# A retention layer and a two-layer network in one kernel: filler matmuls replaced by seven matmuls of the next product, twelve tiles made unit by unit, one scaling moved

## The chip, the cores and the metric

The kernel runs on one core of one Trainium2 chip. The time is device microseconds of one execution; what is compared is the median of several runs. Engines are named as the profile names them: PE (matrix engine; PEld its weight loads), DVE (vector), ACT (scalar), POOL (GpSimd) and SP, which here only issues DMAs.

## The reference

```python
# q, k, v: [4, 8, 768, 64] float32
gamma = 1.0 - 2.0 ** (-5.0 - np.arange(H))
for t in range(S):
    state = gamma * state + outer(k[:, :, t], v[:, :, t])      # per batch and head, 64 x 64
    y[:, :, t] = (1 / sqrt(D)) * (q[:, :, t] @ state)
x = y.transpose(0, 2, 1, 3).reshape(3072, 512)
h = x @ w_in                                                   # [3072, 2048]
g = maximum(h, 0) + alpha * minimum(h, 0)
out = g @ w_out                                                # [3072, 512] float32
```

## The kernel before

The 3072 tokens are cut into 12 *units* of 256 tokens (three to a batch entry, `u`), and two units make a *block* of 512 tokens (`n`, six of them). The recurrence over time is made chunkwise: a unit has two chunks (`c`) of 128 tokens, and all 8 heads are done as 4 pairs.

For a unit the steps are:

- `load` (L149 and L143, issued by SP): keys, queries and values from memory; `hold` makes the next load wait for a named earlier instruction (`held`).
- `rescale` (L169, on DVE or POOL): keys (t = 0) and queries (t = 1) times powers of gamma into the tile `kdq`; `cast_v` (L185): values into `vx`.
- `turn_pe` (L199 on PE, then an ACT copy L205), later `turn_dma`: transposes into `kq`.
- `score_mm` (L284): queries against keys in PSUM tiles `sca` and `scb`; `masks` (L301, later L297, on DVE): causal masking into `m`.
- `sum_mm` (L229): the sum over keys and values of each chunk, in PSUM tile `st`; `state` (DVE L251 or L254, POOL L255) adds it to the running state `tf`, and `state_copy` writes two half copies `tg`, on POOL (letter `g`, L270) or ACT (`a`, L268).
- `out_mm` (L319 with the state, L339 with the scores): the unit's output `y` in two PSUM banks; `take_y` (L357, ACT) evicts them into `xT`, the input of the network.

For a block the network's two products are:

- `ffn1` (L404): 16 tiles of 128 hidden columns; the four matmuls of a tile are 512 tokens wide ("wide"), or, for the first `apart` tiles, the tile is made separately for each unit of the block with 256 tokens ("narrow"), two tiles to a PSUM bank, all those of the first unit ahead of those of the second. ACT (L415, `hm`) and DVE (L417, `gt`) evict: the network's nonlinearity.
- `ffn2` (L442) for block 0: the 64 matmuls of the second product, in four groups of 16, each group reading one quarter of w_out. Later blocks use `ffn2_seven` (L490), a seven-product scheme on 2 x 2 parts with sums of weights (`w_sums`, L375, DVE) and of activations (`g_sums`, L388, DVE).

The order on each engine is the order in which the program is written; no scheduler moves anything. `ffn1` and `ffn2` are generators: `tick(gen, m)` issues the next m matmuls of one, so that matmuls of one stage are laid by hand between steps of another. `keep(m)` issues m matmuls on constants (`kps`, L96) whose result nobody reads. POOL also issues the loads of w_in (`get_wi`, four quarters, L576) and w_out (`get_wo`, four quarters, L580), at their place in its own order. `behind` makes one instruction wait for another.

The places that the change touches are the stretch from unit 1's scores to the start of block 0's first product, block 0's second product (`gen`) with block 1's first product (`half`) laid into it, and POOL's scaling of units 4 and 5.

Of the kernel before, what the change touches and what calls it, by code (L numbers as in the profile page):

```python
# [21 lines left out]
def kernel(  # L22
# [55 lines left out]
    mj = sbp.tile([128, 512], F16, tag="mj", name="mj")[:, 0:384]  # L78
# [14 lines left out]
    def keep(m, bank=7):  # L93
        pt = ps(bank, "kps")
        for i in range(m):
            nc.tensor.matmul(  # L96
                out=pt, lhsT=spin[:, 0:128], rhs=spin, start=True, stop=True
            )
# [92 lines left out]
    def turn_pe(u, hh, bank):  # L191

        kdq, kq, _ = unit(u)
        trb = ps(bank, "trb", F16, 1024)
        n = 0
        for t in range(2):
            for r in range(2):
                for p in (2 * hh, 2 * hh + 1):
                    nc.tensor.transpose(  # L199
                        out=trb[:, n : n + 128],  # L200
                        in_=kdq[:, t, r, 2 * p : 2 * p + 2, :].rearrange("p a d -> p (a d)"),
                        identity=ident,
                    )
                    n += 128
        nc.scalar.activation(  # L205
            out=kq.rearrange("p (x a) i -> p x a i", x=4)[:, :, 2 * hh : 2 * hh + 2, :],
            in_=trb.rearrange("p (x a i) -> p x a i", x=4, a=2),
            func=COPY,
            bias=0.0,
            scale=1.0,  # L210
        )
# [29 lines left out]
    def state(u, c, eng, copy="gg"):  # L241

        state_copy(state_sum(u, c, eng), copy)
# [15 lines left out]
    def state_copy(uct, copy="gg"):  # L259
        if uct is None:  # L260
            return
        u, c, t = uct
        tg = tgbuf[(2 * u + c) % len(tgbuf)]
        tgs[(u, 1) if c == 0 else (u + 1, 0)] = tg
        for a in range(2):
            o, i = tg[rows(a), :, rows(a)], t[rows(a)]
            if copy[a] == "a":
                nc.scalar.activation(out=o, in_=i, func=COPY, bias=0.0, scale=1.0)  # L268
            else:
                nc.gpsimd.tensor_copy(out=o, in_=i)  # L270
# [39 lines left out]
    def out_mm(u, banks, evict=True):  # L310
        _, kq, vx = prepped[u]
        ys = [ps(banks[0], "y0"), ps(banks[1], "y1")]
        inter = [(u, c) in tgs for c in range(2)]
        assert inter == [u % UPB > 0, True]

        for c in range(2):
            for p in range(NP):
                if inter[c]:
                    nc.tensor.matmul(  # L319
                        out=ys[c][:, 128 * p : 128 * p + 128],  # L320
                        lhsT=tgs[u, c][:, p, :],
                        rhs=kq.rearrange("p (t r a) i -> p t r a i", t=2, r=2)[
                            :, 1, :, p, rows(c)
                        ],
                        start=(p == 0),
                        stop=False,
                        skip_group_check=True,
                    )
        for p in range(NP):
            m2s = live[u, p // 2]  # L330
            for r in range(2):
                for c in range(2):
                    for a in range(2):
                        o = ys[c][rows(a), 128 * p : 128 * p + 128]
                        at, n = 256 * r + 128 * (p % 2), 128
                        if u >= SPLIT and r == 1:
                            at, n = 256 + 64 * (p % 2), 64
                            o = o.rearrange("p (r i) -> p r i", r=2)[:, :, 32:64]
                        nc.tensor.matmul(  # L339
                            out=o,  # L340
                            lhsT=vx[rows(c), 2 * p + a, r, :],
                            rhs=m2s[a][rows(c), at : at + n],
                            start=(r == 0 and p == 0 and not inter[c]),
                            stop=(r == 1),
                            skip_group_check=True,
                        )
        live[u] = ys
        if evict:
            take_y(u, (0, 1))

    def take_y(u, cs):
        n, ul = divmod(u, 2)
        if n not in xT:
            xT[n] = sbp.tile([128, 2, NP, U], F16, tag="xT", bufs=2, name=f"xT{n}")
        ys = live[u]
        for c in cs:
            nc.scalar.activation(  # L357
                out=xT[n][:, ul, :, 128 * c : 128 * c + 128].rearrange(
                    "k a (p r) -> k a r p", r=2
                ),  # L360
                in_=ys[c].rearrange("k (a r p) -> k a r p", r=2, p=64),
                func=COPY,
                bias=0.0,
                scale=1.0,
            )
# [24 lines left out]
    def ffn1(n, banks, apart=0):  # L390


        gt = sbp.tile([128, NFT, TB], F16, tag="gt", bufs=2, name=f"gt{n}")
        gts[n] = gt
        turns = [(f, 2, ul, ul + 1) for ul in range(2) for f in range(0, apart, 2)]
        rest = range(apart, NFT)
        if apart == 0:
            rest = [f + x for f in range(HF) for x in (0, HF)]
        turns += [(f, 1, 0, 2) for f in rest]
        for i, (f0, nf, lo, hi) in enumerate(turns):  # L400
            hps = ps(banks[i % len(banks)], "hps").rearrange("p (f t) -> p f t", f=nf)
            for f in range(nf):
                for hp in range(4):
                    nc.tensor.matmul(  # L404
                        out=hps[:, f, :].rearrange("p (u t) -> p u t", t=U),
                        lhsT=w_in_all[:, hp, 128 * (f0 + f) : 128 * (f0 + f) + 128],
                        rhs=xT[n][:, lo:hi, hp, :],
                        start=(hp == 0),
                        stop=(hp == 3),
                    )  # L410
                    if f < nf - 1 or hp < 3:
                        yield
            hm = sbp.tile([128, TB], FP, tag="hm", bufs=3, name="hm")
            hm = hm.rearrange("p (f t) -> p f t", f=nf)
            nc.scalar.activation(out=hm, in_=hps, func=RELU, bias=0.0, scale=-1.0)  # L415
            for f in range(nf):
                nc.vector.scalar_tensor_tensor(  # L417
                    out=gt[:, f0 + f, U * lo : U * hi],
                    in0=hm[:, f, :],
                    scalar=oma_sb[:, f0 + f : f0 + f + 1],  # L420
                    in1=hps[:, f, :],
                    op0=MULT,
                    op1=ADD,
                )
            if n > 0 and f0 in ((HF + 3, NFT - 1) if apart == 0 else (NFT - 1,)):

                lo = 0 if apart or f0 < NFT - 1 else 4
                hi = HF if f0 == NFT - 1 else 4
                g_sums(n, 0, lo, hi)
                g_sums(n, 1, lo, hi)  # L430
            yield
# [134 lines left out]
    def tick(gen, m=10**6):  # L566
        for _ in range(m):
            if next(gen, 1) == 1:
                return
# [4 lines left out]
    def get_wi(lo, hi):  # L574
        s = slice(128 * lo, 128 * hi)
        return nc.gpsimd.dma_start(out=w_in_all[:, :, s], in_=wi[:, :, s])  # L576
# [6 lines left out]
    V, G, A = nc.vector, nc.gpsimd, nc.scalar  # L583
# [3 lines left out]
    load(1, ("k0", "q0", "k1", "q1", "v0", "v1"))  # L587
    V.memset(spin, 1.0)  # L588
    V.memset(mi, 1.0)
    V.memset(mj, 1.0)  # L590
    V.memset(warm, 0.0)
    A.activation(out=warm, in_=warm, func=RELU, bias=0.0, scale=-1.0)

# [55 lines left out]
    take_y(0, (0,))  # L649
    cast_v(G, 1, 0, 4)  # L650
    cast_v(G, 1, 4, 8)
    state_copy(s01)
    score_mm(1, 0, (4, 5))
    masks(1, 0)
    turn_pe(1, 1, 1)
    take_y(0, (1,))
    keep(2, 0)
    sum_mm(1, (6, 7))
    state(1, 0, G, "ga")
    get_wi(8, 12)  # L660
    get_wi(12, 16)
    score_mm(1, 1, (0, 1))
    masks(1, 1)
    state(1, 1, G)
    keep(5, 6)
    get_wo(0)
    rescale(G, 2, 0, 0, 4)
    get_wo(1)
# [1 line left out]
    rescale(G, 2, 0, 4, 8)  # L670
    rescale(G, 2, 1, 4, 8)
    cast_v(G, 2)
    out_mm(1, (4, 5))
    gen = ffn1(0, (2, 3, 6, 7, 0, 1, 2, 3, 6, 7, 4, 5, 0, 1, 2, 3), apart=4)
    tick(gen)


    gen = ffn2(0, (0, 1, 2, 3), parts=4)
    half = ffn1(1, (6, 7, 4, 5, 4, 5, 0, 1, 2, 3, 0, 4, 5, 6, 7, 1), apart=8)
    turn_pe(2, 0, 5)  # L680
    tick(gen, 5)
    score_mm(2, 0, (6, 7))
# [1 line left out]
    load(3, ("k0", "q0", "k1", "q1", "v"))  # L684
    masks(2, 0, (1,))
    turn_pe(2, 1, 4)
    tick(gen, 8)
    score_mm(2, 1, (6, 7))
    sum_mm(2, (5, 4))
    state(2, 0, G, "ga")  # L690
# [10 lines left out]
    w_sums(0, 0, HF)  # L701
    tick(gen, 9)
    out_mm(2, (4, 5))
    tick(gen, 10)
    tick(half, 24)
    turn_pe(3, 0, 6)
    tick(half, 8)
    turn_pe(3, 1, 7)
    tick(gen, 9)
    score_mm(3, 0, (4, 5))  # L710
    masks(3, 0)
    sum_mm(3, (6, 7))
    state(3, 0, G, "ga")
    tick(gen, 8)
    score_mm(3, 1, (4, 5))
    masks(3, 1)
    state(3, 1, G)
    for f in (0, 4):
        for i in range(1, 4):
            gate = w_sums(i, f, f + 4)  # L720
    behind(rescale(G, 4, 0, 0, 8), gate)
    rescale(G, 4, 1, 0, 8)
    rescale(G, 5, 0, 0, 8)
    rescale(G, 5, 1, 0, 8)
    cast_v(G, 4)
# [92 lines left out]
```

## Time and profile before

| | |
|---|---|
| median of 3 runs | 204.94 us (203.43 to 205.25) |
| profiled execution | 203.86 us, span 202.2 us |
| PE busy | 194.0 us (96% of the span) |
| DVE busy | 154.5 us (76%) |
| ACT busy | 101.8 us (50%) |
| POOL busy | 85.2 us (42%) |
| `kps` matmuls (L96), 25 of them | 8.3 us |
| `hps` matmuls (L404), 432 of them | 84.3 us |

The span is the time from the first to the last instruction of the program in one profiled execution; the execution's own time is 1.7 us longer. Shares are of the span. The busy time of PE counts from the start of a matmul to its modelled end, and matmuls overlap, so the spacing of starts says more than the mean duration. In an answer on groups, a row gives line, engine, operation, tile written and tiles read, count, busy us and mean ns of one, and then the engine's idle time ahead of the group with what ended it. In a timeline a row gives the start, the length, and the count of like instructions in a row; square brackets hold the idle time before it and its releaser. In the chain a row gives start, length, and where that time went.

### The profile page before, as it was taken

The page shows a single profiled execution, that of the slowest core. Times are in us where ns is not written, and L with a number is a line of the kernel's source. Part 1 is how long each engine was busy: PE and PEld are TensorE (multiplying, and loading weights), DVE is VectorE, ACT ScalarE, POOL GpSimd, SP SyncE. Part 2 cuts the span into 40 slices and gives each one's busy share as a digit, 9 for nine tenths or more (in the row PEclk, how much of TensorE's full clock was granted, in tenths as well). Part 3 has the DMA queues.
Part 4 walks back from the last instruction along what each step waited for, and adds up shares of the span by engine and source line. Part 5 has one row for each costly group of instructions (what it writes and reads, how often), then busy time and mean ns, then how long its engine had stood idle before and what let it go on. Part 6 is the DMA issues. An engine that isn't in the chain of part 4 may idle for free.

```text
span 202.2 us, 5547 instructions
## 1 busy us (share of the span) xinstructions
PE 194.0 (96%) x2314; PEld 127.8 (63%) x2314; DVE 154.5 (76%) x247; ACT 101.8 (50%) x169; POOL 85.2 (42%) x100
## 2 busy tenths in 40 slices
PE   6688999999999999999999999999999999999993
PEld 2356645566474778744688644788544888544882
DVE  7695887645899999189998289995489984589851
ACT  2455776246387333466454466433466255466321
POOL 5189319390269553980066950076920260000000
PEclk9999999999999999999999999999999999999999
DMA  5999999699997698998995499990570011200014
GB/s 153 312 233 146 194 231 289 185 229 183 333 306 229 143 241 209 245 244 221 201 216 135 152 212 236 208 239 19 179 170 0 3 52 58 104 0 0 9 46 156
DMA packets 77560, 33.95 MB, mean 168 GB/s; under 512 B 43216, under 2 KB 77024, under 8 KB 77536
## 3 DMA queue, kind: packets, MB, share of 16 engines
q1 hardware_dynamic: 73136, 29.37, 54.8%
q0 software_dynamic: 4224, 4.19, 13.6%
q8 instruction: 18, 0.29, 0.6%
q10 hardware_dynamic: 176, 0.04, 0.2%
q14 instruction: 6, 0.05, 0.1%
HBM read 27.31 MB, written 6.29 MB: 166 GB/s over the span
## 4 chain that ended last, share of the span: by engine, by line
PE 81%; DMA 7%; DVE 3%; POOL 3%; issue 2%; SPq 2%; ACT 1%; DVEq 0%; POOLq 0%
PE hps L404 39%; PE ox L490 16%; PE oy L490 11%; PE ops L442 5%; DMA wout<-in_moe_w_out_dram 4%; DMA ks<-in_k_dram 3%; PE y L339 2%; PE y L319 2%; SPq L149 2%; PE sca L284 2%; POOL tf L255 1%; PE st L229 1%; PE oz L490 1%; DVE ss L254 1%; DVE m L301 1%
## 5 line engine op out<-in xcount | busy, mean ns | idle before, releaser
L404 PE MATMUL hps<-xT,win 128*128 128x512 f16 (+1 forms) x432 | 84.3, 355 | 0.0
L417 DVE SCALAR_TENSOR_TENSOR gt<-hm,oma,hps 128x512 f16<-128x512 f32 (+1 forms) x108 | 70.8, 685 | 13.4 <-ACT hm L415 7.7
L415 ACT ACTIVATE hm<-hps 128x512 f32<-128x512 f32 x96 | 57.3, 597 | 33.4 <-PE hps L404 31.2
L404 PEld LDWEIGHTS <-win 128*128 128x128 f16 x432 | 42.2, 98 | 39.9
L490 PEld LDWEIGHTS <-gs 128*128 128x128 f16 x320 | 31.0, 98 | 3.7
L255 POOL TENSOR_TENSOR tf<-ss,tab 128x256 f32<-128x256 f32 x16 | 12.2, 764 | 37.0 <-DVE ss L254 36.0
L490 PEld LDWEIGHTS <-gt 128*128 128x128 f16 x240 | 22.8, 98 | 4.6
L169 POOL TENSOR_TENSOR kdq<-ks,tab 128x1024 f16<-128x1024 f32 (+1 forms) x10 | 17.3, 1727 | 16.7 <-DMA ks<-in_k_dram 11.1
L506 ACT ACTIVATE cu<-ox 128x512 f32<-128x512 f32 (+1 forms) x18 | 9.5, 526 | 29.5 <-PE ox L490 29.4
L511 DVE TENSOR_TENSOR os<-oy,cu 128x512 f32<-128x512 f32 x14 | 9.6, 688 | 17.3 <-PE oy L490 10.2
L270 POOL CAST tg<-tf 64x256 f16<-64x256 f32 x29 | 14.0, 482 | 19.6 <-DVE tf L251 18.2
L169 POOL TENSOR_TENSOR kdq<-qs,tab 128x1024 f16<-128x1024 f32 (+1 forms) x13 | 21.1, 1623 | 0.6 <-DMA qs<-in_q_dram 0.4
L490 PE MATMUL ox<-wsum,gs 128*128 128x256 f16 x160 | 19.1, 273 | 0.0
L357 ACT ACTIVATE xT<-y 128x512 f16<-128x512 f32 x24 | 16.2, 741 | 5.0 <-PE y L339 4.8
L442 PE MATMUL ops<-wout,gt 128*128 128x512 f16 x64 | 15.2, 380 | 0.2 <-DMA wout<-in_moe_w_out_dram 0.2
L185 POOL CAST vx<-vs 128x1024 f16<-128x1024 f32 (+1 forms) x13 | 12.5, 971 | 4.6 <-DMA vs<-in_v_dram 4.6
L388 DVE TENSOR_TENSOR gs<-gt 128x1024 f16<-128x1024 f16 (+1 forms) x14 | 13.1, 934 | 0.3
L268 ACT ACTIVATE tg<-tf 64x256 f16<-64x256 f32 x11 | 4.6, 414 | 15.4 <-POOL tf L255 10.2
L205 ACT ACTIVATE kq<-trb 128x1024 f16<-128x1024 f16 x8 | 8.2, 1023 | 6.3 <-PE trb L199 6.2
L301 DVE TENSOR_TENSOR m<-sca,mi 128x512 f16<-128x512 f32 x12 | 8.2, 685 | 3.0 <-PE scb L284 3.0
L490 PE MATMUL ox<-wout,gt 128*128 128x256 f16 x80 | 10.4, 274 | 0.0
L96 PE MATMUL kps<-spin 128*128 128x512 f16 x25 | 8.3, 471 | 1.8 <-DVE spin L588 1.5
(54 smaller groups left out, 187.9 us busy)
## 6 DMA issues: line engine op xcount, KB each, us to landing
out_dram<-os SPq DMA_DIRECT2D x21, 256.0 KB, 2.8
qs<-in_q_dram SPq DMA_DIRECT2D x8, 512.0 KB, 5.6
ks<-in_k_dram SPq DMA_DIRECT2D x24, 128.0 KB, 3.3
vs<-in_v_dram SPq DMA_DIRECT2D x24, 128.0 KB, 4.9
ks<-in_k_dram SPq DMA_DIRECT2D x8, 256.0 KB, 5.2
qs<-in_q_dram SPq DMA_DIRECT2D x8, 256.0 KB, 5.2
win<-in_moe_w_in_dram POOLq DMA_DIRECT2D x4, 512.0 KB, 7.3
wout<-in_moe_w_out_dram POOLq DMA_DIRECT2D x4, 512.0 KB, 8.5
```

Of the source, the lines that this page charges most:

```text
L169: return eng.tensor_tensor(out=kdq[:, t, :, h0:h1, :].rearrange("p r h d -> p h r d"), in0=staged[u]["kq"[t]][:, h0:h1, :].rearrange("p h ...
L185: eng.tensor_copy(out=o, in_=i)
L255: eng.tensor_tensor(out=t, in0=ss, in1=dec, op=MULT)
L270: nc.gpsimd.tensor_copy(out=o, in_=i)
L301: i = nc.vector.tensor_tensor(out=m2.rearrange("p (r a i) -> p r a i", r=2, a=2), in0=live[u, hh][a].rearrange("p (r a i) -> p r a i", r=2 ...
L357: nc.scalar.activation(out=xT[n][:, ul, :, 128 * c : 128 * c + 128].rearrange("k a (p r) -> k a r p", r=2), in_=ys[c].rearrange("k (a r p) ...
L388: return nc.vector.tensor_tensor(out=o, in0=a, in1=b, op=op)
L404: nc.tensor.matmul(out=hps[:, f, :].rearrange("p (u t) -> p u t", t=U), lhsT=w_in_all[:, hp, 128 * (f0 + f) : 128 * (f0 + f) + 128], rhs=x ...
L415: nc.scalar.activation(out=hm, in_=hps, func=RELU, bias=0.0, scale=-1.0)
L417: nc.vector.scalar_tensor_tensor(out=gt[:, f0 + f, U * lo : U * hi], in0=hm[:, f, :], scalar=oma_sb[:, f0 + f : f0 + f + 1], in1=hps[:, f, :],
L442: nc.tensor.matmul(out=opss[tq], lhsT=gt[:, ft, 128 * tq : 128 * tq + 128], rhs=w_out_all[:, ft, :], start=(ft == 0), stop=(ft == NFT - 1),)
L490: nc.tensor.matmul(out=o[1][m], lhsT=lhs(f, m), rhs=rhs(f), start=(first and f == 0 and (m == 0 or o[0] is None)), stop=(f == HF - 1), ski ...
```

## The change

- Ahead of unit 1's product the five constant matmuls `keep(5, 6)` go. In their place stand the first seven matmuls of block 0's first product, all narrow and of unit 0.
- Of unit 1's output one half is evicted by DVE instead of ACT (`take_y` gets an engine).
- The two state copies of unit 0's second chunk are made by ACT instead of POOL, and later in the program; the third quarter of w_in is issued by POOL in their place, earlier than before. The memset of `mj` goes from DVE to POOL.
- Block 1's first product makes 12 tiles unit by unit instead of 8, with one bank of the list changed; 16 of its narrow matmuls are laid ahead of unit 3's scores.
- The matmuls of block 0's second product are laid out otherwise around unit 2: five ahead of its first transpose, six instead of eight after the second, seven instead of ten after its output.
- The scaling of unit 4's keys on POOL moves from behind the last of the `w_sums` to just after unit 3's first state; the scaling of unit 4's queries is now the one that waits for the `w_sums`.

```diff
-    def take_y(u, cs):
+    def take_y(u, cs, eng=None):
...
+            if eng is not None:
+                eng.tensor_copy(out=o, in_=i)
+                continue
...
-    V.memset(mj, 1.0)
+    G.memset(mj, 1.0)
...
     cast_v(G, 1, 4, 8)
-    state_copy(s01)
+    get_wi(8, 12)
     score_mm(1, 0, (4, 5))
     masks(1, 0)
     turn_pe(1, 1, 1)
     take_y(0, (1,))
+    state_copy(s01, "aa")
     keep(2, 0)
     sum_mm(1, (6, 7))
     state(1, 0, G, "ga")
-    get_wi(8, 12)
     get_wi(12, 16)
     score_mm(1, 1, (0, 1))
     masks(1, 1)
     state(1, 1, G)
-    keep(5, 6)
+    gen = ffn1(0, (2, 3, 6, 7, 0, 1, 2, 3, 6, 7, 4, 5, 0, 1, 2, 3), apart=4)
+    tick(gen, 7)
     get_wo(0)
...
-    out_mm(1, (4, 5))
-    gen = ffn1(0, (2, 3, 6, 7, 0, 1, 2, 3, 6, 7, 4, 5, 0, 1, 2, 3), apart=4)
+    out_mm(1, (4, 5), evict=False)
+    take_y(1, (0,))
+    take_y(1, (1,), V)
     tick(gen)
...
     gen = ffn2(0, (0, 1, 2, 3), parts=4)
-    half = ffn1(1, (6, 7, 4, 5, 4, 5, 0, 1, 2, 3, 0, 4, 5, 6, 7, 1), apart=8)
+    half = ffn1(1, (6, 7, 4, 5, 4, 6, 0, 1, 2, 3, 0, 4, 5, 6, 7, 1), apart=12)
+    tick(gen, 5)
     turn_pe(2, 0, 5)
     tick(gen, 5)
     score_mm(2, 0, (6, 7))
...
     turn_pe(2, 1, 4)
-    tick(gen, 8)
+    tick(gen, 6)
     score_mm(2, 1, (6, 7))
...
     out_mm(2, (4, 5))
-    tick(gen, 10)
+    tick(gen, 7)
     tick(half, 24)
     turn_pe(3, 0, 6)
     tick(half, 8)
     turn_pe(3, 1, 7)
+    tick(half, 16)
     tick(gen, 9)
     score_mm(3, 0, (4, 5))
     masks(3, 0)
     sum_mm(3, (6, 7))
     state(3, 0, G, "ga")
+    rescale(G, 4, 0, 0, 8)
     tick(gen, 8)
...
-    behind(rescale(G, 4, 0, 0, 8), gate)
-    rescale(G, 4, 1, 0, 8)
+    behind(rescale(G, 4, 1, 0, 8), gate)
     rescale(G, 5, 0, 0, 8)
```

More of the change, by code (lines that the diff above doesn't have):

```diff
@@ L356, in take_y @@
         for c in cs:
+            o = xT[n][:, ul, :, 128 * c : 128 * c + 128].rearrange("k a (p r) -> k a r p", r=2)
+            i = ys[c].rearrange("k (a r p) -> k a r p", r=2, p=64)
+            if eng is not None:
+                eng.tensor_copy(out=o, in_=i)
+                continue
             nc.scalar.activation(
[L358 to L361, printed above, removed]
+                out=o,
+                in_=i,
                 func=COPY,
```

## The prediction

> **What bounds the kernel now.** I read the page's spans, busy times and chain first, then the time between PE's instructions stretch by stretch, then the landings of the weights that the moved matmuls read.
>
> ```profile
> span 202.2 us, 5547 instructions
> PE 194.0 (96%) x2314; PEld 127.8 (63%) x2314; DVE 154.5 (76%) x247; ACT 101.8 (50%) x169; POOL 85.2 (42%) x100
> PE 81%; DMA 7%; DVE 3%; POOL 3%; issue 2%; SPq 2%; ACT 1%; DVEq 0%; POOLq 0%
> ...
> 33.17:47.94 14.77, 14.53 (x185) 9.39 (x182) 9.22 (x16) 7.40 (x12) 8.59 (x10) 1.00 0.99 202
> 67.63:84.40 16.77, 16.34 (x306) 14.17 (x304) 13.11 (x19) 6.50 (x11) 8.90 (x10) 1.00 0.94 228
> ```
>
> The first three lines are the page's span, PE's busy share and the chain that ended last; the other two are stretches of the busy times (start and end, length, then PE, PEld, DVE, ACT, POOL, the granted clock, the DMA share and GB/s). PE is the bound. Once it has work it hardly stops: it is idle 0.24 us of the 14.77 in which block 0's second product runs, and 0.43 of the 16.77 that follow block 1's first product. So a new order of the same matmuls can only win what PE idles, or what it spends on filler. The diff touches three places: the filler before unit 1's product, the second product of block 0, and the tail of block 1's first product.
>
> **Place 1, the filler before unit 1's product.** Timeline and chain around it, and the load of the first quarter of w_in (POOL's issue, then the time to its landing):
>
> ```profile
> 16.38 0.22 PE L284 MATMUL scb<-kq 64*64 64x128 f16 x1
> 17.02 0.61 POOL L255 TENSOR_TENSOR tf<-ss,tab 128x256 f32<-128x256 f32 x1 [0.25 <-DVE ss L254]
> 17.66 0.41 ACT L268 ACTIVATE tg<-tf 64x256 f16<-64x256 f32 x1 [0.89 <-POOL tf L255]
> 17.69 0.39 POOL L270 CAST tg<-tf 64x256 f16<-64x256 f32 x1
> 18.03 1.55 POOL L576 DMA_DIRECT2D win<-in_moe_w_in_dram  x2
> ...
> 16.92 1.24 PE kps L96 x5
> 18.16 0.45 PE y L319 x8
> 18.61 0.57 PE y L339 x32
> 19.18 13.97 PE hps L404 x80
> ...
> 10.52 0.94 POOL L576 DMA_DIRECT2D win<-in_moe_w_in_dram  x1
> DMA to landing us min/median/max: 7.6/7.6/7.6
> ```
>
> The scores of unit 1 end at 16.38 + 0.22 = 16.60. Unit 1's product (L319, L339) needs the state copies tg, the last of which ends at 17.69 + 0.39 = 18.08. Between them stand five matmuls on constants (kps), 1.24 us, until 18.16. The change takes these out and puts in the first seven matmuls of block 0's first product, half as wide. Their price, from other rows of the same shape:
>
> ```profile
> 43.20 2.78 PE L404 MATMUL hps<-xT,win 128*128 128x256 f16 x24
> 45.83 0.62 PE L199 MATMUL trb<-mi,kdq 128*128 128x128 f16 x8
> 47.16 0.61 PE L199 MATMUL trb<-mi,kdq 128*128 128x128 f16 x8
> 47.94 2.10 PE L442 MATMUL ops<-wout,gt 128*128 128x512 f16 x9 [0.17 <-DMA wout<-in_moe_w_out_dram]
> 84.40 13.81 PE hps L404 x64
> ```
>
> 24 narrow ones take 45.83 - 43.20 = 2.63 us, 0.110 each; a wide one takes 13.81 / 64 = 0.216. Seven are 0.77 us that need not run later, and if they fitted between 16.60 and 18.08 that would be the gain. But they read columns of w_in whose load is issued at 10.52 and lands 7.6 us later, at 18.1. Nothing in the diff stands ahead of that issue that could bring it forward: before it POOL only gains the memset of mj (below). So the new order is: wait from 16.60 to 18.12, seven matmuls to 18.89, the product 0.45 + 0.57 = 1.02 to 19.91, the other 73 matmuls 13.97 - 0.77 = 13.20 to 33.11. Before, they end at 19.18 + 13.97 = 33.15. **Gain: 0.04 us.** The wait for the weights takes the place of the filler; behind it on PE stands unit 1's product, and ACT and DVE wait for that to evict it. The bounds are 0 (each 0.1 us that the load lands later is paid in full) and 0.77 (it lands by 17.3). I take 0.04, from the row.
>
> Around it, at nothing while the cover holds. The state copies of unit 0 go from POOL to ACT, two of 0.41 us, into ACT's idle 0.89; without that hole, the copy at 17.66 and with it unit 1's product would be late by the overhang. In POOL's place the third w_in load is issued before the tf at 17.02 instead of at 18.03: it is 0.78 us (1.55 for two) and takes the place of two POOL copies of 0.39, so POOL reaches tf as before. One half of unit 1's eviction goes to DVE; the trace has no such copy there, the nearest rows are the two forms of the group below, 0.48 and 0.75 us. I take 0.75. Both halves are then done at 19.91 + 0.75 = 20.7, and the first matmul that reads them comes after nine more narrow ones, at 19.91 + 0.99 = 20.9. The memset of mj on POOL:
>
> ```profile
> 2.08 0.29 POOL L594 TENSOR_SCALAR_AFFINE_SELECT mi<-mi 128x128 f16<-128x128 f16 x1 [1.57 <-DVE mi L589]
> ```
>
> POOL sits idle 1.57 us ahead of this and waits for DVE's memset of mi, which stands ahead of the one that moves. The new one would have to exceed 1.57 us to cost; it sets 128x384 elements where the 128x128 select takes 0.29, so three times that, 0.87, is my estimate. DVE's next work needs landed keys, so what it saves is worth 0 to the path.
>
> **Place 2, the wait for w_out.** In the row of 47.94 PE waits 0.17 us for the third quarter of w_out. What issues it:
>
> ```profile
> 39.72 0.80 POOL L580 DMA_DIRECT2D wout<-in_moe_w_out_dram  x1
> DMA to landing us min/median/max: 8.2/8.2/8.2
> ```
>
> It lands at 47.9. Three matmuls of the second product now stand ahead of the sums of unit 2 that did not (5 + 5 + 6 against 5 + 8), and POOL issues this load after the state of unit 2. So the issue goes back 3 x 0.216 = 0.65 us, to 40.4, the landing to 48.55, and SP's loads of units 4 and 5, which are held behind it, go back too. Against that, 16 narrow matmuls (1.75 us) now stand after the transposes of 47.16 and ahead of the matmul that waits. It comes at 47.94 - 0.17 + 1.75 = 49.52, with 0.97 us to spare. **Gain: 0.17 us**, bounds 0 and 0.17 while the landing slips by less than 0.97 more. The keys of unit 3 are issued later as well (two groups of five matmuls now stand ahead of the first scores where one did), which is what could make it slip. Unit 2's eviction stays just covered:
>
> ```profile
> 40.46 0.64 PE L339 MATMUL y<-m,vx 64*64 64x128 f16 x32
> 41.13 1.34 ACT L357 ACTIVATE xT<-y 128x512 f16<-128x512 f32 x2 [1.37 <-PE y L339]
> ```
>
> It ends 41.13 + 1.34 - 41.10 = 1.37 us after the product; ten matmuls (2.16 us) covered it, now seven do (1.52).
>
> **Place 3, twelve tiles unit by unit.** Four more tiles are made in halves: 16 wide matmuls become 32 narrow ones, 16 x (2 x 0.110 - 0.216) = 0.06 us on PE. **Loss: 0.05.** For DVE:
>
> ```profile
> L417 DVE SCALAR_TENSOR_TENSOR gt<-hm,oma,hps 128x512 f16<-128x512 f32 x84 | 60.6, 745 | 8.8 <-ACT hm L415 3.2
> L417 DVE SCALAR_TENSOR_TENSOR gt<-hm,oma,hps 128x256 f16<-128x256 f32 x24 | 10.3, 476 | 4.6 <-ACT hm L415 4.5
> ```
>
> By these means four tiles cost 4 x (2 x 476 - 745) = 0.83 us more; 24 halves are busy only 10.3 us together, 0.43 each, so 0.46 is the lower end. A pair of half tiles is then 0.86 to 0.95 us of DVE against 8 x 0.110 = 0.88 on PE, so DVE about keeps pace, and the last four tiles (0.745 against 0.865) let it catch up before the end. I take 0.
>
> **Place 3, unit 4's keys.** The 16 narrow matmuls also push the masks of unit 3 and the w_sums back by 1.75 - 0.17 = 1.58 us, while what is left of block 1's product shrinks as much. POOL's scalings of units 4 and 5 hang on the last w_sums:
>
> ```profile
> 47.91 0.37 SPq L149 DMA_DIRECT2D ks<-in_k_dram  x1
> DMA to landing us min/median/max: 4.2/4.2/4.2
> ...
> 52.12 0.39 POOL L270 CAST tg<-tf 64x256 f16<-64x256 f32 x1 [6.69 <-DVE tf L251]
> 54.66 0.93 POOL L255 TENSOR_TENSOR tf<-ss,tab 128x256 f32<-128x256 f32 x1 [2.15 <-DVE ss L254]
> 59.08 1.90 POOL L169 TENSOR_TENSOR kdq<-ks,tab 128x1024 f16<-128x1024 f32 x1 [1.88 <-issue]
> 66.50 2.02 POOL L185 CAST vx<-vs 128x1024 f16<-128x1024 f32 x2
> ...
> 68.43 0.63 PE L229 MATMUL st<-vx,kdq 64*64 64x64 f16 x44
> ```
>
> POOL runs from 59.08 to 68.52, PE's sums of units 4 and 5 from 68.43. Left as it was, that row of work would start at 60.66 and end at 70.1, 1.5 us or more behind PE. The scaling of unit 4's keys, 1.90 us, now goes into POOL's idle 2.15: after the tg of 52.12 (now 53.7 to 54.1) and before the tf of 54.66 (now 56.24). It ends at 56.0, and its keys land at 47.91 + 4.2 + 0.65 = 52.8. So the rest ends at 70.1 - 1.86 (the starts in this row are 1.86 apart on average: (66.50 - 59.08) / 4) = 68.24 against a need of 68.3 for the first and 68.6 for the last sums. **Cost: 0**, bounds 0 and 0.3.
>
> One wait is left as it stands:
>
> ```profile
> 75.32 0.41 PE L339 MATMUL y<-m,vx 64*64 64x128 f16 x15 [0.43 <-DVE m L301]
> ```
>
> DVE gets there from the last evicted tile by the same instructions, so it moves with PE.
>
> **The sum**: 0.04 + 0.17 - 0.05 = 0.16 us less. The profiled execution took 203.86 us (span 202.2 and 1.7 around it), so 203.7. The median of the runs shown, 204.94, is 1.1 above it; off that, **204.8**.
>
> **The rivals.**
>
> *The weights are early after all.* If the load of w_in lands by 17.3, the whole 0.77 is won: 204.94 - 0.16 - 0.73 = 204.05. For it: one execution shows one landing, and the queue is shared with the loads of unit 1. Against: 0.8 us is a tenth of its whole flight. Chance 0.22.
>
> *The clock falls in the new hole (slower).* Without the filler PE stands still from 16.60 to 18.12.
>
> ```profile
> 1.52 4.24 PE L96 MATMUL kps<-spin 128*128 128x512 f16 x10 [1.52 <-DVE spin L588]
> 5.43:8.84 3.41, 2.28 (x36) 1.30 (x34) 1.75 (x4) 1.02 (x1) 0.00 (x0) 1.00 1.06 314
> 15.67:19.08 3.41, 2.86 (x92) 1.92 (x80) 2.13 (x5) 1.51 (x3) 3.03 (x7) 1.00 1.09 155
> ```
>
> Ten such matmuls at the start took 4.24 us, 0.42 each, and five at 16.92 took 1.24: PE starts at half rate. Back at half rate for as long as those ten, it would lose 4.24 - 10 x 0.216 = 2.1 us: 204.94 + 2.1 - 0.16 = 206.9. It decides as soon as the hole counts as rest. Against: PE was busy 2.28 of 3.41 us in the early stretch without falling; the hole, from 16.92 where the filler began, leaves 2.86 - 1.2 = 1.66 in its stretch, about half. Chance 0.1. The Trainium skill (TensorE: Matmul & The Clock Gate, Part 1: The HAM clock gate) says that the clock halves after an idle window of about 3.4 us, by which a hole of 1.5 would be harmless; its section on a second failure mode says that frequent short idles between groups make the clock swing, by which this rival holds. No run here shows which.
>
> *The late loads overtake the cover (slower by a little).* If w_out's third quarter slips 1 to 2 us more, or POOL's row ends late by its 0.3, PE waits 0.1 to 1.0: 204.9 to 205.8. For it: the issue goes back and meets later key loads. Against: 0.97 to spare. Chance 0.18.
>
> The forecast keeps 0.5.
>
> **How the numbers follow.** A measurement of this kernel can tell about 1% (2.05 us) from no change; the runs before spread over 1.8. No case for faster reaches 2.05, only a spread of runs on the early weights: 0.06. The clock case lies at the bound, so half of it and some of the late loads together: 0.1. Within 1%: 0.84. The range goes from the early weights less the spread of the runs below the median, 203.0, to the clock case, 206.9.
>
> **What would show it.** Right: no kps at 16.9, seven hps from 18.1 with an idle of about 1.5 us put down to win; the last matmul of block 0's first product at 33.1; no wait at the third w_out quarter, which lands near 48.6; a POOL scaling of ks between 54 and 56; the 0.43 us wait still there. Wrong: seven hps before 17.5 (early weights), hps 0.2 us apart after 18 (clock), a wait on wout at 49.5, or sums of unit 4 that wait for POOL.

## The result, and the profile after

| | before | changed |
|---|---|---|
| median (22 runs each) | 203.70 us (202.71 to 205.25) | 202.83 us (201.88 to 206.15) |
| ratio | | 0.9944, 95% interval 0.9921 to 0.9967 |
| profiled execution | 203.86 us, span 202.2 | 203.15 us, span 201.4 |

By the ratio the changed kernel is faster by 0.56%, 1.1 us; the forecast was 0.16 us, within what counts as no change here. The ratio leaves out three runs of the changed kernel in which PE's granted clock fell (0.989 to 0.992, 205.0 to 206.15 us); over all runs the medians lie 0.87 us apart. In a repeat of the changed kernel beside other kernels the ratio was 0.9936 (0.9897 to 0.9974).

The page of the changed kernel (span, busy times, chain that ended last):

```profile
span 201.4 us, 5574 instructions
PE 193.2 (96%) x2325; PEld 129.0 (64%) x2325; DVE 155.3 (77%) x251; ACT 102.0 (51%) x170; POOL 85.1 (42%) x99
PE 86%; DMA 6%; DVE 2%; POOL 2%; SPq 1%; issue 1%; ACT 0%; POOLq 0%
```

PE's busy time fell by 0.8 us although it issues eleven matmuls more on balance: five wide filler matmuls are gone. Place 1 in the timeline of PE (first two rows: the last of unit 1's scores, then the seven) and in the chain:

```profile
15.93 0.22 PE L284 MATMUL scb<-kq 64*64 64x128 f16 x1
17.72 0.94 PE L407 MATMUL hps<-xT,win 128*128 128x256 f16 x7 [1.57 <-DMA win<-in_moe_w_in_dram]
...
10.06 7.61 DMA win<-in_moe_w_in_dram
17.67 0.05 issue
17.72 0.94 PE hps L407 x7
18.66 0.45 PE y L319 x8
19.10 0.57 PE y L339 x32
19.67 13.20 PE hps L407 x73
```

This is the forecast's picture: the load is 7.61 us on its way, PE is idle 1.57 us for it, then come the seven, unit 1's product and 73 more in 13.20 us. Only the seven take 0.94 us in the chain where the forecast has 0.77. In this execution place 1 wins nothing. PE's timeline at place 2 and at its wait for a mask of DVE, then, for place 3, POOL's and the first sums of units 4 and 5:

```profile
46.85 0.61 PE L199 MATMUL trb<-mi,kdq 128*128 128x128 f16 x8
47.30 1.91 PE L407 MATMUL hps<-xT,win 128*128 128x256 f16 x16
49.04 2.11 PE L445 MATMUL ops<-wout,gt 128*128 128x512 f16 x9
74.72 0.41 PE L339 MATMUL y<-m,vx 64*64 64x128 f16 x15 [0.43 <-DVE m L301]
```

```profile
53.59 1.90 POOL L169 TENSOR_TENSOR kdq<-ks,tab 128x1024 f16<-128x1024 f32 x1
55.76 0.93 POOL L255 TENSOR_TENSOR tf<-ss,tab 128x256 f32<-128x256 f32 x1 [0.28 <-DVE ss L254]
60.19 1.90 POOL L169 TENSOR_TENSOR kdq<-qs,tab 128x1024 f16<-128x1024 f32 x1 [1.88 <-issue]
65.77 2.02 POOL L185 CAST vx<-vs 128x1024 f16<-128x1024 f32 x2
...
67.83 0.63 PE L229 MATMUL st<-vx,kdq 64*64 64x64 f16 x44
```

The group of 49.04 has no bracket: no wait for w_out is left here. Unit 4's keys are scaled in POOL's hole from 53.59, and POOL's row ends at 67.79, just ahead of PE's sums of units 4 and 5 from 67.83. PE's wait of 0.43 us for DVE stands as before. So each step can be seen, and yet the two traces explain only part of 1.1 us. Of the 0.71 us between the spans 0.45 lie ahead of every difference on the path: unit 1's scores end at 15.93 + 0.22 = 16.15 here and at 16.60 before. The experiments had to tell whether that, place 1 or place 2 made the median.

### The profile page after: what moved, and what is told of

Read it like the earlier page. It is cut to its first block, busy times and chain, and to the rows that moved or that the text cites. A ratio compares the mean times of both kernels' runs of the same rounds, so it can differ in the third digit from the quotient of the medians.

```text
span 201.4 us, 5574 instructions
## 1 busy us (share of the span) xinstructions
PE 193.2 (96%) x2325; PEld 129.0 (64%) x2325; DVE 155.3 (77%) x251; ACT 102.0 (51%) x170; POOL 85.1 (42%) x99
## 4 chain that ended last, share of the span: by engine, by line
PE 86%; DMA 6%; DVE 2%; POOL 2%; SPq 1%; issue 1%; ACT 0%; POOLq 0%
PE hps L407 41%; PE ox L493 16%; PE oy L493 11%; PE ops L445 7%; DMA win<-in_moe_w_in_dram 4%; PE y L339 3%; DMA vs<-in_v_dram 3%; PE y L319 2%; PE sca L284 2%; SPq L149 1%; PE st L229 1%; PE trb L199 1%; PE oz L493 1%; DVE gs L391 1%; POOL tf L255 1%
## 5 line engine op out<-in xcount | busy, mean ns | idle before, releaser
L407 PEld LDWEIGHTS <-win 128*128 128x128 f16 x448 | 43.5, 98 | 40.2 <-DMA win<-in_moe_w_in_dram 1.7
L493 PEld LDWEIGHTS <-gt 128*128 128x128 f16 x240 | 22.8, 98 | 4.6
L270 POOL CAST tg<-tf 64x256 f16<-64x256 f32 x27 | 13.2, 491 | 19.6 <-DVE tf L251 18.3
L362 ACT ACTIVATE xT<-y 128x512 f16<-128x512 f32 x23 | 15.7, 743 | 6.0 <-PE y L339 5.8
L268 ACT ACTIVATE tg<-tf 64x256 f16<-64x256 f32 x13 | 5.3, 414 | 14.0 <-POOL tf L255 9.0
L445 PEld LDWEIGHTS <-gt 128*128 128x128 f16 x64 | 5.8, 98 | 6.0
```

Source lines behind the costliest of these rows:

```text
L407: nc.tensor.matmul(out=hps[:, f, :].rearrange("p (u t) -> p u t", t=U), lhsT=w_in_all[:, hp, 128 * (f0 + f) : 128 * (f0 + f) + 128], rhs=x ...
L445: nc.tensor.matmul(out=opss[tq], lhsT=gt[:, ft, 128 * tq : 128 * tq + 128], rhs=w_out_all[:, ft, :], start=(ft == 0), stop=(ft == NFT - 1),)
L493: nc.tensor.matmul(out=o[1][m], lhsT=lhs(f, m), rhs=rhs(f), start=(first and f == 0 and (m == 0 or o[0] is None)), stop=(f == HF - 1), ski ...
```

## The experiments

Theory A: the gain lies at place 2, where a wait for w_out costs more than its idle time shows. Theory B, later sharpened to D: at place 1, in executions in which w_in lands earlier than in the two profiled ones. Theory C: in the start and the early loads. The traces also serve as a sample of when w_in lands.

**One place at a time.** `e1_seven` is the kernel before with place 1 alone:

```diff
-    state_copy(s01)
+    get_wi(8, 12)
...
+    state_copy(s01, "aa")
...
-    get_wi(8, 12)
...
-    keep(5, 6)
+    gen = ffn1(0, (2, 3, 6, 7, 0, 1, 2, 3, 6, 7, 4, 5, 0, 1, 2, 3), apart=4)
+    tick(gen, 7)
...
-    out_mm(1, (4, 5))
-    gen = ffn1(0, (2, 3, 6, 7, 0, 1, 2, 3, 6, 7, 4, 5, 0, 1, 2, 3), apart=4)
+    out_mm(1, (4, 5), evict=False)
+    take_y(1, (0,))
+    take_y(1, (1,), V)
```

> Kernel before with place 1 alone: the seven matmuls in the filler's stead, half of unit 1's eviction on DVE, the state copies on ACT and the third w_in load issued early; memset and second product as before. Theory A (the gain lies at place 2, where a wait for w_out costs more than its idle time shows): no gain here, 0.0 to 0.2 us slower, and in its trace the seven start within 0.1 us of the landing of w_in, some 1.5 us after the scores of unit 1. Theory B (the gain lies at place 1, in executions in which w_in lands early): 0.5 to 0.8 us faster, and the idle ahead of the seven under 1.0 us. Theory C (the gain lies in the early loads and the start): as much faster as the kernel with the early loads alone.

Measured: 0.9959 (0.9935 to 0.9982), 0.8 us faster. In its trace PE waits for the load only 0.57 us:

```profile
16.83 0.94 PE L407 MATMUL hps<-xT,win 128*128 128x256 f16 x7 [0.57 <-DMA win<-in_moe_w_in_dram]
17.61 0.61 PE L319 MATMUL y<-kq,tg 128*128 128x128 f16 x8
```

The gain and the idle are those of theory B; theory A's "no gain here" falls.

`e2_second` is the kernel before with everything from the start of `ffn2(0)` on as in the changed kernel (places 2 and 3; some of its lines):

```diff
-    half = ffn1(1, (6, 7, 4, 5, 4, 5, 0, 1, 2, 3, 0, 4, 5, 6, 7, 1), apart=8)
+    half = ffn1(1, (6, 7, 4, 5, 4, 6, 0, 1, 2, 3, 0, 4, 5, 6, 7, 1), apart=12)
...
+    tick(half, 16)
     tick(gen, 9)
...
+    rescale(G, 4, 0, 0, 8)
```

> Kernel before with places 2 and 3 alone: twelve tiles unit by unit, the second product laid out anew, unit 4's keys scaled early. Theory A: most of the measured gain, 0.3 to 1.1 us faster; no wait at the third w_out quarter in its trace. Theory B: 0.1 to 0.2 us faster at most. Theory C: the same.

Measured: 0.9972 (0.9948 to 0.9997), 0.57 us faster (0.06 to 1.1). Its trace shows no wait at the third w_out quarter. The prediction gives these places 0.17 - 0.05 = 0.12 us, which lies inside that interval; so A is not refuted for its part, and not shown by this time alone.

`e3_early` has only the moved loads, copies and memset:

```diff
-    V.memset(mj, 1.0)
+    G.memset(mj, 1.0)
...
-    state_copy(s01)
+    get_wi(8, 12)
...
+    state_copy(s01, "aa")
...
-    get_wi(8, 12)
```

> Kernel before with only the state copies on ACT, the third w_in load issued early and the memset of mj on POOL; filler and second product as before. Theory A and theory B: within 0.2 us of the kernel before. Theory C: 0.4 us or more faster, with the first transposes or the start of block 0's first product earlier by that in its trace.

Measured: 0.9987 (0.9963 to 1.0011), not told from nothing. Theory C has no support. But its trace shows no wait at the third w_out quarter either, nor does that of `e1_seven`, which moves the same loads and copies and keeps the old second product. So the moves, or chance in the landing, may share in what place 2 wins. The 0.8 of `e1_seven` contains them too, and the two parts together (0.41% and 0.28%) come to a little more than the whole.

**The kernels themselves again.** `e0_before` and `e10_before` are the kernel before, unchanged, and `e9_after` the changed kernel, unchanged, one profiled execution each; `e7_after` is the changed kernel once more, in 12 runs.

> The kernel before once more, for a second trace of it. If the 0.45 us by which the changed kernel's profiled execution was ahead at the scores of unit 1 are chance of the first loads, this trace lies anywhere between or beyond the two at that point, and its wait for the third w_out quarter differs from 0.17 us. If they belong to the change, this trace has the scores of unit 1 end near 16.6 us again.

> The kernel before for one more trace. Theory D: whenever w_in lands, block 0's first product ends 16.55 us after the scores of unit 1, since the filler and the state copies stand ahead of it; the PE work behind it takes 165.4 us plus the wait for the third w_out quarter, 0.2 to 0.45 us.

> The changed kernel for one more trace of the landing of w_in. Theory D: from the scores of unit 1 to the landing 0.3 to 0.6 us (two times in three) or 1.5 us, and the end of block 0's first product is 15.2 us plus that wait behind the scores, whichever it is.

> The changed kernel once more, beside the other three. Theory D: w_in lands within 0.7 us of the scores of unit 1 in its trace, the idle ahead of the seven is under 0.8 us instead of 1.57, and the median is 0.8 to 1.3 us below the kernel before. Theory A: the idle is near 1.5 us again and the gain is that of the second product alone, 0.3 to 0.6 us.

Measured: unit 1's scores end at 16.04 in `e0_before` and at 15.87 in `e10_before`, so the 0.45 us at the start is chance of the first loads and not the change. At the third w_out quarter the kernel before is not idle in `e0_before` and waits longest in `e10_before`:

```profile
46.52 0.61 PE L199 MATMUL trb<-mi,kdq 128*128 128x128 f16 x8
47.63 2.10 PE L442 MATMUL ops<-wout,gt 128*128 128x512 f16 x9 [0.49 <-DMA wout<-in_moe_w_out_dram]
```

The median of `e7_after` is 202.12 us, 1.45 under the kernel before beside it (1.3 by the ratio, 0.9936), and PE is idle 0.55 us ahead of the seven: theory D. The chain of `e7_after` beside that of the changed kernel's first trace above:

```profile
9.87 6.67 DMA win<-in_moe_w_in_dram
16.54 0.05 issue
16.59 0.94 PE hps L407 x7
17.52 0.46 PE y L319 x8
17.99 0.57 PE y L339 x32
18.56 13.20 PE hps L407 x73
```

The load takes 6.67 us instead of 7.61, unit 1's scores end 0.12 earlier, and block 0's first product ends at 31.75 instead of 32.87. From these traces, each read in the same way: S is the end of unit 1's scores, L the landing of the first quarter of w_in, F the end of block 0's first product, Z the end of PE's last matmul.

| kernel | L - S | F - S | Z - F |
|---|---|---|---|
| filler: first trace of before | 1.50 | 16.54 | 165.78 |
| filler: `e0_before` | 0.26 | 16.56 | 165.57 |
| filler: `e10_before` | 0.14 | 16.54 | 166.19 |
| filler: `e3_early` | 0.27 | 16.56 | 165.36 |
| filler: `e2_second` | 0.60 | 16.56 | 165.35 |
| seven: `e1_seven` | 0.53 | 15.72 | 165.36 |
| seven: first trace of changed | 1.52 | 16.72 | 165.35 |
| seven: `e7_after` | 0.51 | 15.72 | 165.36 |
| seven: `e9_after` | 0.80 | 15.99 | 165.39 |
| seven: `e8_two` (below) | 1.17 | 16.36 | 165.36 |

With the filler F - S is 16.55 whenever the weights land; with the seven it is 15.2 plus L - S, and 15.72 at best among these. `e9_after` was expected to keep to that sum, and does; its landing, 0.80, lies between the two values that were expected. The gain is 0.84 us at L - S = 0.5, nil at 1.35, and -0.17 at 1.5. Of the twelve traces in which the quarter is loaded whole (these ten, `e4_hole` with 1.56 and `e6_keys` with 0.51), eight have L - S at 0.8 or less: both traces that the comparison began with belong to the four others. What differs is the load itself: unit 1's scores end 6.1 to 6.4 us behind its issue in all twelve, while from issue to landing it takes 6.22 to 7.03 us in the eight and 7.25 to 7.64 in the four. Stretches of the changed kernel's first trace, then the same of `e7_after` (the last two columns are the DMA share and GB/s):

```profile
13.00:14.00 1.00, 0.84 (x49) 0.58 (x41) 1.00 (x2) 1.00 (x2) 1.00 (x2) 1.00 1.09 167
14.00:15.00 1.00, 1.00 (x17) 0.58 (x11) 1.00 (x3) 0.63 (x2) 1.00 (x3) 1.00 1.19 174
```

```profile
13.00:14.00 1.00, 0.92 (x51) 0.67 (x40) 1.00 (x3) 0.99 (x2) 1.00 (x2) 1.00 1.23 203
14.00:15.00 1.00, 1.00 (x19) 0.53 (x20) 1.00 (x3) 0.65 (x2) 1.00 (x3) 1.00 1.22 196
```

In the two stretches the core moves 167 and 174 GB/s instead of 203 and 196, at a DMA share of 1.09 and 1.19 against 1.23 and 1.22; why, the runs do not show. The last column of the table is place 2 but for 0.1 us or less: 0.2 to 0.8 us that all traces with its rearrangement or with the early loads lack. At the upper end, in `e10_before`, it is nearly twice the most that was expected of that trace.

**Nothing in the hole.** `e4_hole` is the changed kernel without the seven ahead:

```diff
     gen = ffn1(0, (2, 3, 6, 7, 0, 1, 2, 3, 6, 7, 4, 5, 0, 1, 2, 3), apart=4)
-    tick(gen, 7)
```

> The changed kernel with nothing in the filler's place: the five constant matmuls gone, the seven issued after unit 1's product with the rest. Theory D (in most executions w_in lands within 0.7 us of the scores of unit 1, so that the seven fill a wait of 1.4 us that unit 1's product has anyway): slower than the changed kernel by 0.5 to 0.8 us in the median. Theory A (place 1 is worth nothing, as in the profiled execution of the changed kernel): the same as the changed kernel within 0.2 us. The clock rival: with PE at rest for 1.4 us in every execution, some of them with a granted clock under 0.995 and 2 us longer; if the hole does not count as rest, no more of those than of the kernel before.

Measured: 202.86 us, ratio 0.9964 (0.9941 to 0.9986), against 202.12 and 0.9936 of the changed kernel beside it: 0.74 us in the median, theory D's figure, though the intervals of the two ratios overlap. The kernel with places 2 and 3 and the filler (`e2_second`) has 0.9972, so in the median the empty hole costs no more than the filler. But in the profiled execution the clock falls. Stretches before, during and after, the granted clock being the third figure from the end:

```profile
14.80:18.23 3.43, 2.05 (x81) 1.47 (x84) 2.43 (x5) 2.61 (x5) 3.04 (x7) 1.00 1.16 166
18.23:21.65 3.42, 3.42 (x39) 2.38 (x28) 1.20 (x3) 1.34 (x2) 2.15 (x4) 0.50 1.16 175
21.65:25.06 3.41, 3.41 (x26) 2.42 (x25) 2.73 (x8) 2.15 (x4) 0.00 (x0) 1.00 1.21 205
```

```profile
17.11 0.85 PE L319 MATMUL y<-kq,tg 128*128 128x128 f16 x8 [1.08 <-ACT tg L268]
...
17.58 0.38 PE y L319 x4
17.96 0.73 PE y L339 x32
18.69 15.42 PE hps L407 x80
```

Right behind the hole the granted clock is 0.50 for 3.4 us, and the 80 matmuls take 15.42 us instead of the 13.97 of before.

**The first load cut in two**, `e5_split`:

```diff
-    get_wi(0, 4)
+    get_wi(0, 2)
     rescale(G, 1, 1, 0, 4)
+    get_wi(2, 4)
...
-    held.append(get_wi(4, 8))
-    load(2, ("k0", "q0", "k1", "q1", "v"))
...
     cast_v(G, 1, 4, 8)
-    get_wi(8, 12)
+    held.append(get_wi(4, 8))
+    load(2, ("k0", "q0", "k1", "q1", "v"))
...
+    get_wi(8, 12)
     get_wi(12, 16)
```

The second quarter, unit 2's loads and the third quarter move back with it.

> The changed kernel with the first w_in load cut in two: the two tiles that the seven read come alone, the other two after the first scaling of unit 1's queries, the second quarter after unit 1's values are cast. Theory D: the seven wait for no load in any trace; the median 0.1 to 0.4 us lower than the changed kernel's, and the spread of its runs smaller at the top. Theory A: no difference. Against both: POOL is 0.8 us longer before unit 1's state, and if that is on the path, 0.3 to 0.8 us slower.

Measured: 202.36 us, 0.9927 (0.9898 to 0.9955). The median is 0.24 above that of the changed kernel beside it, where 0.1 to 0.4 below was expected, and the ratio is a little under its 0.9936: the two are not told apart. Its highest run is 203.02 against 204.58. The seven wait for no load, but PE does, twice, further on:

```profile
16.33 0.92 PE L407 MATMUL hps<-xT,win 128*128 128x256 f16 x7 [0.21 <-ACT xT L362]
21.61 0.60 PE L407 MATMUL hps<-xT,win 128*128 128x512 f16 x2 [0.23 <-DMA win<-in_moe_w_in_dram]
38.08 1.24 PE L445 MATMUL ops<-wout,gt 128*128 128x512 f16 x5 [0.44 <-DMA wout<-in_moe_w_out_dram]
```

The wait is moved, not removed: w_in's second quarter and w_out's second quarter come later.

**Unit 4's keys back behind the w_sums**, `e6_keys`:

```diff
-    rescale(G, 4, 0, 0, 8)
     tick(gen, 8)
...
-    behind(rescale(G, 4, 1, 0, 8), gate)
+    behind(rescale(G, 4, 0, 0, 8), gate)
+    rescale(G, 4, 1, 0, 8)
```

> The changed kernel with the scaling of unit 4's keys behind the last of the w_sums again, ahead of unit 4's queries. By the prediction's own step POOL's row of work ends about 1.9 us later, at 69.6 on the changed kernel's trace, and PE waits 1.2 to 1.6 us for it at the sums of units 4 and 5: 1.2 to 1.6 us slower than the changed kernel. If DVE's work after block 1's first product hides part of it (PE waits there 0.43 us anyway), 0.5 to 1.1 us slower.

Measured: 205.53 us, 1.0081 (1.0046 to 1.0116), 3.4 us above the changed kernel beside it, twice the larger expectation, with a granted clock of 0.989 to 0.992 in all five runs.

```profile
67.48 0.45 PE L229 MATMUL st<-vx,kdq 64*64 64x64 f16 x32 [0.80 <-POOL vx L185]
69.46 0.37 PE L229 MATMUL st<-vx,kdq 64*64 64x64 f16 x11 [1.53 <-POOL vx L185]
```

```profile
66.25:69.66 3.41, 1.08 (x51) 0.78 (x51) 3.27 (x4) 0.19 (x1) 3.15 (x3) 1.00 0.68 154
69.66:73.07 3.41, 3.41 (x58) 2.58 (x51) 3.28 (x6) 0.38 (x1) 1.96 (x4) 0.50 0.77 176
```

PE waits 0.80 and 1.53 us for POOL's two casts, and then the clock is at half for 3.41 us, which costs half of that, 1.7; the later wait of 0.43 us for DVE is gone. So the cover was needed: without it places 2 and 3 together lose.

**Two filler matmuls ahead of the seven**, `e8_two`, meant to shorten the hole:

```diff
+    keep(2, 2)
     gen = ffn1(0, (2, 3, 6, 7, 0, 1, 2, 3, 6, 7, 4, 5, 0, 1, 2, 3), apart=4)
     tick(gen, 7)
```

> The changed kernel with two of the constant matmuls back, ahead of the seven. Theory D: they take 0.43 us of a wait that is at least 0.5 us long, so the median stays within 0.15 us of the changed kernel's (0.5 to 0.7 % under the kernel before). Clock rival: if it is the hole that makes the clock fall in some executions of the changed kernel (and of the one with nothing in the filler's place), the shorter hole shows fewer runs with a granted clock under 0.995, none of some twelve. If the filler delays the seven, 0.2 to 0.4 us slower.

Measured: 202.31 us, 0.9955 (0.9928 to 0.9981), 0.45% under the kernel before where 0.5 to 0.7 was expected: not told from the changed kernel. None of its 12 runs has a granted clock under 0.995. Of the 34 timed runs of the changed kernel four have, of 12 of `e4_hole` one, of 12 of `e1_seven`, which has the same hole, none; of the 73 runs of the kernel before that were timed beside the experiments one has, of the 24 of `e2_second` and `e3_early`, both with the filler, none. That points to the hole, but the numbers are small. No version tried is shown to beat the changed kernel.

## Why the prediction was wrong, step by step

- **Place 1, "I take 0.04, from the row": the step that failed.** The mechanism was right, the wait for the weights does take the filler's place. But one execution's landing, 18.1, was taken for the kernel's, and it was a late one: 1.50 us behind the scores, where eight of twelve traces have 0.8 or less. In the traces of kernels with the seven that land so, the term is 0.56 to 0.84 instead of 0.04; place 1 alone, with the moved loads, gave 0.8 us (`e1_seven`, 0.4 to 1.3), and the seven against an empty hole 0.74 with overlapping intervals (`e4_hole`). The rival "the weights are early after all" had it, with a chance of 0.22 where about two in three was due. Its objection, that 0.8 us is a tenth of the flight, was no argument: flights of 6.67 and 7.61 us both occur. Nor is a shared queue the reason: on the page the loads of w_in stand under POOL's queue and those of the units under SP's.
- **The sum at place 1 was off even for a landing at 18.1.** It starts unit 1's product at 18.16, the modelled end of the filler, but prices the seven by the spacing of starts, 0.77. From start to modelled end they take 0.94; counted alike, that landing costs 0.13 instead of winning 0.04. The first trace of the changed kernel, landing 1.52 us behind the scores, shows a loss of 0.17.
- **Place 2, 0.17: too small.** The gap in the row runs from the modelled end of the last transpose. By starts it is more: the transposes of 47.16 are followed after 0.78 us by the waiting matmul, those of 46.85 after 0.45 by the next, so 0.33 was lost. And it varies with the landing of w_out: in `e10_before` the idle is 0.49 us. From the table the whole stretch behind F is 0.2 to 0.8 us shorter; how much of that the rearrangement won and how much the early loads, the runs do not tell apart. The predicted slip of the issue to 40.4 is 39.95 with the 0.45 by which this execution is ahead; the trace has 40.06, and no wait took its place.
- **Place 3, narrow matmuls and DVE**: right. Block 1's remaining product runs from 58.17 to 66.87, 8.70 us; 48 narrow and 16 wide at the prediction's prices are 8.7. PE's wait of 0.43 us for DVE stayed.
- **POOL's cover**: right that it is needed; "1.5 us or more behind PE" was short of the 3.4 us that its loss costs, since the clock falls on top.
- **The clock rival**: its mechanism exists, read in two traces, and three of the 22 runs of the changed kernel have a mean granted clock of 0.989 to 0.992 like those two; it did not set the median. By the Trainium skill's rule (TensorE: Matmul & The Clock Gate, Part 1: The HAM clock gate) it takes an idle window of about 3.4 us. The length agrees with the 3.41 and 3.42 us at half clock here, but the condition does not: PE was busy for 2.05 of 3.43 us in `e4_hole` before the clock fell.
- **The range and the signs.** 202.83 lies below 203.0, the low end. The median of before over more runs is 203.70 instead of the 204.94 on which the range stood, so 1.2 of the 2.0 us between 204.8 and 202.83 are the base and 0.7 the two terms. The low end does not follow from its own words either: the early weights, 204.05, less the spread of the runs below the median, 204.94 - 203.43 = 1.51, is 202.5.

## What to carry to other kernels

A landing read from one trace is one draw. Where a step is worth its full price or nothing by a microsecond of a transfer, take more than one trace of the landing, or give the two outcomes their own chances, before one row sets the sum. Filler ahead of a wait is the first place to put real work, as long as that work's own inputs are there; and a wait's price is read from start to start, not from the idle time alone.

## What the runs showed of the hardware

The clock can fall without a stretch of full rest. Stretches of 3.41 us, in step with the clock's own changes in each trace: it fell after PE had been busy for 1.08 us (`e6_keys`) and 2.05 us (`e4_hole`, whose row above is 3.43 long), then ran at 0.50 for one such stretch and came back. But it held after 1.90 us in the changed kernel's first trace, in the stretch that has most of its hole of 1.57 us, and after 1.78 us near the end of `e5_split`:

```profile
14.02:17.43 3.41, 1.90 (x62) 1.20 (x58) 2.82 (x6) 3.00 (x6) 3.04 (x6) 1.00 1.10 160
17.43:20.85 3.42, 3.13 (x59) 2.69 (x60) 1.25 (x3) 1.27 (x4) 3.06 (x6) 1.00 1.14 155
...
196.25:199.66 3.41, 1.78 (x17) 1.34 (x14) 0.69 (x1) 0.77 (x2) 0.00 (x0) 1.00 0.64 226
199.66:201.26 1.60, 0.00 (x0) 0.00 (x0) 0.00 (x0) 0.00 (x0) 0.00 (x0) 1.00 0.03 9
```

So the busy time of a stretch, as the profile counts it, does not decide by itself; what does stays open.

The same load of 512 KB, issued at the same place of the program, took 6.22 to 7.64 us from issue to landing over twelve traces.
